# Moving the four block-diagonal copies of each q chunk from VectorE to SBUF-to-SBUF transfers, in an attention and MLP kernel with a fixed SyncE queue order

## The chip, the cores and the metric

The kernel runs on one core of one Trainium2 chip. The metric is the device time of one execution in microseconds (us), as the median of several runs. All timed runs quoted here were in the fast state; on one core that means that no run was more than 1.5% above the fastest run of the same kernel. (m1_shapes alone was run once, so its state is unknown; nothing is concluded from its time.) Ratios are computed as the mean time of one kernel's fast runs over that of the kernel before in the same rounds, so a ratio isn't quite the ratio of the medians quoted beside it. PE is TensorE, DVE is VectorE, ACT is ScalarE, SP is SyncE, which issues nearly all transfers here.

## The reference

Two layers, each of a local dilated attention and a token-mixing MLP, both with a residual (S = 2048 tokens, D = 1024, 32 heads of 32, window 8, dilation 2, F = 3584):

```python
def _A_ref(x, wqkv, wo):                       # attention
    H = 32; Dh = D // H; W, dil = 8, 2
    q, k, v = split_heads(x @ wqkv)            # cut: reshapes
    idx = pos[:, None] - dil * arange(W)[None, :]
    logits = einsum("bhsd,bhswd->bhsw", q, k[idx]) * Dh ** -0.5   # cut: mask of idx < 0
    o = einsum("bhsw,bhswd->bhsd", softmax(logits), v[idx])
    return merge_heads(o) @ wo

def _B_ref(x, w1, b1, w2, b2):                 # MLP over the tokens
    u = gelu(einsum("bsd,sf->bdf", layernorm(x), w1) + b1)
    return (einsum("bdf,fs->bds", u, w2) + b2).transpose(0, 2, 1)

for _ in range(2):
    x = x + _A_ref(layernorm(x), A_wqkv, A_wo)
    x = x + _B_ref(layernorm(x), B_w1, B_b1, B_w2, B_b2)
```

## The kernel before

One attention layer is cut into 16 units: a group of four heads (128 partitions, 32 per head) times one parity of the tokens. A unit has two visits (b = 0 and b = 1) of some 4.45 us each: 16 score matmuls, the value matmuls of the visit before, and two projection chunks for the next unit. In b = 0 these are the two q chunks, in b = 1 the two k chunks. Each q chunk is cast from PSUM to a tile `qs` by ACT, and then each head's 32 partitions are put into the head's own slot of `qB`. All else in `qB` is zero, so one matmul gives the scores of four heads apart.

```python
    def qk_chunk(u, wts, part, n):
        ...                                    # cut: 8 matmuls of 128x512 into ps
        ls = slice(n * 512, (n + 1) * 512)
        if part:
            nc.scalar.copy(out=kT[u % 2][:, ls], in_=ps[:])
        else:
            qs = x2("qs", [P, 512])            # shared pool of 6 buffers
            nc.scalar.copy(out=qs[:], in_=ps[:])
            for h in range(HG):                # 4 heads
                hp = slice(h * DH, (h + 1) * DH)
                nc.vector.tensor_copy(out=qB[u % 2][hp, h, ls], in_=qs[hp, :])
        return mm

    def scores(u, b):
        q, k = qB[u % 2], kT[u % 2]
        ...
        for i in range(HB):                    # 4 blocks of 128 tokens
            lo = (b * HB + i) * P
            for r in range(P // KG):           # 4 groups of 32 keys
                mm = nc.tensor.matmul(dst, lhsT=k[:, lo + r * KG:lo + (r + 1) * KG],
                                      rhs=q[:, :, lo + r * KG:lo + r * KG + GW], ...)   # GW = 40
        ...

    def out_proj(c, i, oT, wo, res, dst, h2):
        xr = x2("xr")                          # same pool
        nc.sync.dma_start(out=xr[:], in_=res(c, i))
        xn = x2("xn")                          # same pool
        for n in range(NDC):
            ...                                # 8 matmuls
            nc.vector.tensor_tensor(out=xn[:, xs_], in0=ps[:], in1=xr[:, xs_], op=ALU.add)
        nc.sync.dma_start(out=rows(dst, c, i), in_=xn[:])
        ...                                    # layernorm of xn into h2

        for vis in range(2 * NU):              # 32 visits of a layer
            u, b = divmod(vis, 2)
            if b == 0 and u + 1 < NU and (u + 1) % (2 * DIL) == 0:
                load_qk(...)                   # two loads of 512 KB
            if vis == 2 * NU - 6:
                wo = load_wo()                 # four loads of 512 KB
            in_order(scores, u, b)
            if vis:
                in_order(values, *divmod(vis - 1, 2), v, oT)
            for n in range(2):
                if u + 1 < NU:
                    in_order(qk_chunk, u + 1, wts, *chunks[2 * b + n])
                else:
                    in_order(out_proj, 0, 2 * b + n, oT, wo, res, xa[li], h2)
```

The last of the 16 matmuls of visit b = 0 reads columns 480 to 520, and so the first eight columns of the second q chunk. The second chunk is thus wanted when the unit starts, not half a unit later.

The softmax here doesn't subtract the row's maximum and nothing guards it: scores larger than these inputs give would overflow.

Of the kernel before, what the change touches and what calls it, by code (L numbers as in the profile page):

```python
# [12 lines left out]
BF16 = mybir.dt.bfloat16  # L13

P = 128
# [3 lines left out]
DIL = 2  # L19
# [6 lines left out]
def kernel(  # L26
# [15 lines left out]
    nc = tc.nc  # L42
# [9 lines left out]
    NG = D // P  # L52
    HG = P // DH
    NDC = D // 512
    FB = 256
# [13 lines left out]
    def pool(name, bufs, **kw):  # L69
        return ctx.enter_context(tc.tile_pool(name=name, bufs=bufs, **kw))  # L70
# [6 lines left out]
    wp = pool("wp", 9)  # L77
    x2p = pool("x2p", 6)
    pcp = pool("pcp", 2)
    dram = pool("dram", 1, space=bass.MemoryType.DRAM)  # L80
    psm = pool("psm", 2, space=bass.MemoryType.PSUM)
    pss = pool("pss", 2, space=bass.MemoryType.PSUM)
# [20 lines left out]
    def x2(name, shape=None, dt=BF16):  # L103
        return x2p.tile(shape or [P, D], dt, name=name, tag="x2")

    def wt_(name, shape):
        return wp.tile(shape, BF16, name=name, tag="w")
# [41 lines left out]
    qB = [pers.tile([P, HG, SC + W], BF16, name=f"qB{n}") for n in range(2)]  # L149
# [15 lines left out]
    wo_v = A_wo.rearrange("(g p) n -> p g n", p=P)  # L165
    w1_v = B_w1.rearrange("(i p c) f -> c p i f", p=P, c=DIL)
# [31 lines left out]
    last = {}  # L198

    def chain_(eng, f, *args):  # L200
        with tc.issue_after(last[eng].ins) if eng in last else nullcontext():
            last[eng] = f(*args)
# [138 lines left out]
    def load_qk(g2, ts):  # L341
        for part in range(2):
            ts[part] = wt_("wqk", [P, KD, 256])
            r = nc.sync.dma_start(out=ts[part][:], in_=wq_v[:, :, part * D + g2 * 256:part * D + (g2 + 1) * 256])
        return r

    def qk_chunk(u, wts, part, n):
        g, c = divmod(u, DIL)
        ps = m_tile()
        lo = c * SC + n * 512  # L350
        for kt in range(KD):
            mm = nc.tensor.matmul(ps[:], lhsT=wts[part][:, kt, (g % 2) * P:(g % 2 + 1) * P], rhs=hT[:, kt, lo:lo + 512],  # L352
                                  start=(kt == 0), stop=(kt == KD - 1))
        ls = slice(n * 512, (n + 1) * 512)
        if part:
            nc.scalar.copy(out=kT[u % 2][:, ls], in_=ps[:])  # L356
        else:
            qs = x2("qs", [P, 512])
            nc.scalar.copy(out=qs[:], in_=ps[:])  # L359
            for h in range(HG):  # L360
                hp = slice(h * DH, (h + 1) * DH)
                nc.vector.tensor_copy(out=qB[u % 2][hp, h, ls], in_=qs[hp, :])  # L362
        return mm

    last_pe = [None]
# [61 lines left out]
        nc.vector.tensor_tensor(out=oT[g][:, lo:lo + HB * P], in0=acc[:, 0, :], in1=rd[:], op=ALU.mult)  # L427
        return mm

    def load_wo():  # L430
        tiles = []
        for n in range(NDC):
            tiles.append([])
            for hf in range(2):
                t = wt_("wo", [P, NG // 2, 512])
                nc.sync.dma_start(out=t[:], in_=wo_v[:, hf * (NG // 2):(hf + 1) * (NG // 2), n * 512:(n + 1) * 512])
                tiles[n].append(t)
        return tiles

    def out_proj(c, i, oT, wo, res, dst, h2):  # L440
        xr = x2("xr")
        nc.sync.dma_start(out=xr[:], in_=res(c, i))
        xn = x2("xn")
        for n in range(NDC):
            ps = m_tile()
            xs_ = slice(n * 512, (n + 1) * 512)
            for g in range(NG):
                mm = nc.tensor.matmul(ps[:], lhsT=oT[g][:, cols(c, i)], rhs=wo[n][g // 4][:, g % 4, :],  # L448
                                      start=(g == 0), stop=(g == NG - 1))
            nc.vector.tensor_tensor(out=xn[:, xs_], in0=ps[:], in1=xr[:, xs_], op=ALU.add)  # L450
        nc.sync.dma_start(out=rows(dst, c, i), in_=xn[:])
        h2[c][i] = vhp.tile([P, D], BF16, name="h2", tag="vh")
        mean, rs = stats(xn, 1.0 + EPS, eps2)
        norm_act(h2[c][i][:], xn[:], mean, rs)
        return mm

    order = [(c, i) for c in range(DIL) for i in range(NI)]

    def load_w1(fb):
        tiles = []  # L460
        for c in range(DIL):
            t = wt_("w1", [P, NI, FB])
            nc.sync.dma_start(out=t[:], in_=w1_v[c, :, :, fb * FB:(fb + 1) * FB])
            tiles.append(t)
        return tiles

    def gemm1(fb, h2, g):
        wt = load_w1(fb)
        pairs = []
        g[fb] = gop.tile([P, GF, D], BF16, name="g", tag="go")  # L470

        def mm(fl, k):
            c, i = order[k]
            for dc in range(NDC):
                nc.tensor.matmul(pairs[fl][0][dc], lhsT=wt[c][:, i, fl * P:(fl + 1) * P],  # L475
                                 rhs=h2[c][i][:, dc * 512:(dc + 1) * 512], start=(k == 0), stop=(k == NT - 1))

        def gelu(fl):
            ft = fb * GF + fl
            aps, t = pairs[fl]  # L480
            if t is not None:
                nc.scalar.activation(out=g[fb][:, fl, :].rearrange("p (n d) -> p n d", n=2), in_=t[:],  # L482
                                     func=ACT.Gelu_apprx_tanh, bias=b1_sb[:, ft:ft + 1])
            else:
                for dc in range(NDC):
                    nc.scalar.activation(out=g[fb][:, fl, dc * 512:(dc + 1) * 512], in_=aps[dc],
                                         func=ACT.Gelu_apprx_tanh, bias=b1_sb[:, ft:ft + 1])

        for fl in range(GF):
            pairs.append(pair(fb * GF + fl))  # L490
        if fb == 0:
            for k in range(NT):
                for fl in range(GF):
                    mm(fl, k)
            for fl in range(GF):
                gelu(fl)
        else:
            for fl in range(GF):
                for k in range(NT):
                    mm(fl, k)  # L500
                gelu(fl)

    def load_w2(i):
        tiles = []
        for n in range(NW2):
            t = wt_("w2", [P, HF, 256])
            nc.sync.dma_start(out=t[:], in_=w2_v[:, n * HF:(n + 1) * HF, i * 256:(i + 1) * 256])
            tiles.append(t)
        return tiles
# [19 lines left out]
    NU = NG * DIL  # L529
    for li in range(2):  # L530
        first = li == 0
        v = [[None] * NI for _ in range(DIL)]
        for c, i in order:
            v[c][i] = vhp.tile([P, D], BF16, name="v", tag="vh")
        wv = load_wv()
        if first:
            start_up(v, wv)
            wts = [None, None]
            chain_("SP", load_qk, 0, wts)
            res = lambda c, i: xin_v[c, i]  # L540
        else:
            fill_wv(wv, 0)
            fill_wv(wv, 1)
            wts = [None, None]
            load_qk(0, wts)
            for i in range(NI):
                for c in range(DIL):
                    v_proj(v, c, i, wv, (0, 1))
            res = lambda c, i: rows(xb, c, i)
        oT = [gop.tile([P, S], BF16, name="oT", tag="go") for _ in range(NG)]  # L550
        h2 = [[None] * NI for _ in range(DIL)]
        chunks = [(0, 0), (0, 1), (1, 0), (1, 1)]
        last_pe[0] = None
        for part, n in chunks:
            in_order(qk_chunk, 0, wts, part, n)
        wo = None
        for vis in range(2 * NU):
            u, b = divmod(vis, 2)
            if b == 0 and u + 1 < NU and (u + 1) % (2 * DIL) == 0:
                wts = [None, None]  # L560
                load_qk((u + 1) // (2 * DIL), wts)
            if vis == 2 * NU - 6:
                wo = load_wo()
            in_order(scores, u, b)
            if vis:
                in_order(values, *divmod(vis - 1, 2), v, oT)
# [3 lines that stand above are left out]
                else:  # L570
                    in_order(out_proj, 0, 2 * b + n, oT, wo, res, xa[li], h2)
        in_order(values, NU - 1, 1, v, oT)
        for c, i in order[4:]:
            out_proj(c, i, oT, wo, res, xa[li], h2)
        g = [None] * NFB
        for fb in range(NFB):
            gemm1(fb, h2, g)
        if first:
            ln_exp_table()
        for i in range(NI):  # L580
            w2t = load_w2(i)
            for c in range(DIL):
                gemm2(c, i, w2t, g, xa[li], rows(xb, c, i) if first else out_v[c, i], first)

# [29 lines left out]
```

## Time and profile before

| | before |
|---|---|
| time, median of 3 runs (lowest to highest) | 1305.25 us (1304.77 to 1306.91) |
| span of the profiled run, granted TensorE clock | 1303.6 us, 1.0 |
| PE busy | 1278.7 us (98%) |
| DVE busy | 454.4 us (35%), 72.6 us of it the copies into qB |
| PE waits for DVE xn in the output projection | 7.3 us |

From the page of the kernel before: the busy time of each engine (us, share of the span, instructions), and the first line of the chain of work that ended last.

```profile
PE 1278.7 (98%) x8258; PEld 592.9 (45%) x8414; DVE 454.4 (35%) x971; ACT 372.4 (29%) x628; POOL 2.4 (0%) x15
...
PE 95%; DMA 2%; DVE 2%; issue 1%; ACT 1%; DVEq 0%; SPq 0%
```

PE is both the busiest engine and nearly all of the chain. What the other engines do costs nothing until PE waits for it. Three groups of instructions follow (line, engine, operation, output<-inputs, shapes, count | busy us, mean ns of one | idle us of the engine before them).

```profile
L352 PE MATMUL m<-hT,wqk 128*128 128x512 bf16 x963 | 223.4, 379 | 6.2 <-issue 4.6
...
L362 DVE COPY qB<-qs 32x512 bf16<-32x512 bf16 x256 | 72.6, 284 | 77.5 <-ACT qs L359 73.4
...
L380 PE MATMUL s<-qB,kT 128*32 128x160 bf16 x1024 | 29.5, 235 | 0.1
```

The score matmuls are 29.5 us of work and never wait (0.1 us). The "issue" idle time of the first line is no wait at all: 963 of 1024 matmuls have a record in this trace, and a missing record looks like a gap. From the view of PE's waits, by what it waited for (us in total, times, longest us):

```profile
PE m L448 <- DVE xn L450: 7.3, 6, 2.0
...
PE m L352 <- issue: 4.6, 29, 0.2
```

The timeline around the longest of these waits (start us, duration us, engine, work, [idle before <- what ended it]):

```profile
226.02 2.82 SPq L442 DMA_DIRECT2D xr<-in_A_x_dram  x2
...
230.66 1.29 DVE L450 TENSOR_TENSOR xn<-m,xr 128x512 bf16<-128x512 f32 x2 [2.64 <-DMA xr<-in_A_x_dram]
...
231.41 0.81 PE L448 MATMUL m<-wo,oT 128*128 128x512 bf16 x3 [1.98 <-DVE xn L450]
```

The residual tile xr is asked for when its tile starts; DVE sits idle 2.64 us for it, PSUM isn't emptied, and PE loses 1.98 us. Finally the timeline of an ordinary unit. The q chunks are cast, DVE copies them, and the next unit's scores come long after.

```profile
119.69 0.58 ACT L359 CAST qs<-m 128x512 bf16<-128x512 f32 x1 [0.35 <-PE m L352]
...
120.89 2.38 DVE L362 COPY qB<-qs 32x512 bf16<-32x512 bf16 x8
...
121.42 0.58 ACT L359 CAST qs<-m 128x512 bf16<-128x512 f32 x1 [1.14 <-PE m L352]
...
125.72 0.46 PE L380 MATMUL s<-qB,kT 128*32 128x160 bf16 x16
```

The eight copies end at 120.89 + 2.38 = 123.27, and the scores that read them start at 125.72: the copies have 2.45 us to spare.

### The profile page before, as it was taken

The numbers are of one execution on the slowest core, as the hardware profiler recorded it, in microseconds if no ns is written. First come the engines' busy times: TensorE is split into PE (matmuls) and PEld (weight loads), VectorE is DVE, ScalarE is ACT, GpSimd is POOL, SyncE is SP. The second block draws the span as 40 slices with busy tenths as digits, with TensorE's granted clock in tenths as the row PEclk, the third lists the DMA queues.
The fourth block names the chain that finished last, engine by engine and source line by source line (L and its number), as shares of the span: only waits on it lengthen the run. The fifth ranks groups of instructions, "written<-read, shape, count | busy, mean of one in ns | idle before, by whom it ended". The sixth has DMA issues, their size and how long they took to land.

```text
span 1303.6 us, 19189 instructions
## 1 busy us (share of the span) xinstructions
PE 1278.7 (98%) x8258; PEld 592.9 (45%) x8414; DVE 454.4 (35%) x971; ACT 372.4 (29%) x628; POOL 2.4 (0%) x15
## 2 busy tenths in 40 slices
PE   9999999999999999999999999999999999999998
PEld 4444444444444444444444444444444444444443
DVE  7468888820000013322300788888000000111111
ACT  5356665431111110000023666654211111000000
POOL 0000000000000000000000000000000000000000
PEclk9999999999999999999999999999999999999999
DMA  8620113452223236465432101034522222334330
GB/s 236 134 76 18 34 34 105 139 154 82 80 65 88 60 94 153 123 153 146 129 81 64 35 23 29 18 130 155 145 65 81 81 60 73 109 105 137 113 92 32
DMA packets 195812, 121.58 MB, mean 93 GB/s; under 512 B 37904, under 2 KB 177424, under 8 KB 195728
## 3 DMA queue, kind: packets, MB, share of 16 engines
q1 hardware_dynamic: 195728, 120.36, 32.6%
q8 instruction: 65, 1.06, 0.3%
q14 instruction: 19, 0.16, 0.0%
HBM read 96.48 MB, written 16.78 MB: 87 GB/s over the span
## 4 chain that ended last, share of the span: by engine, by line
PE 95%; DMA 2%; DVE 2%; issue 1%; ACT 1%; DVEq 0%; SPq 0%
PE m L352 17%; PE s L518 15%; PE s L475 15%; PE acc L475 7%; PE m L475 7%; PE m L518 7%; PE acc L518 7%; PE m L448 6%; PE m L337 4%; PE m L255 4%; PE s L380 2%; PE acc L408 1%; DMA xr<-in_A_x_dram 1%; PE acc L412 1%; DMA xr<-xb 1%
## 5 line engine op out<-in xcount | busy, mean ns | idle before, releaser
L518 PEld LDWEIGHTS <-w 128*128 128x128 bf16 x1792 | 175.3, 98 | 211.4
L475 PEld LDWEIGHTS <-w 128*128 128x128 bf16 x1792 | 175.3, 98 | 211.4
L352 PE MATMUL m<-hT,wqk 128*128 128x512 bf16 x963 | 223.4, 379 | 6.2 <-issue 4.6
L521 DVE SCALAR_TENSOR_TENSOR xo<-s,b_sb,xs 128x512 bf16<-128x512 f32 x32 | 24.0, 751 | 539.8 <-PE s L518 533.5
L475 PE MATMUL s<-h,w 128*128 128x512 bf16 x878 | 201.3, 379 | 0.8
L518 PE MATMUL s<-g,w 128*128 128x512 bf16 x884 | 199.3, 379 | 0.7
L352 PEld LDWEIGHTS <-wqk 128*128 128x128 bf16 x1024 | 95.2, 98 | 118.0 <-issue 10.7
L388 DVE TENSOR_TENSOR Pm<-pc,band 32x640 bf16<-32x640 bf16 x256 | 123.7, 483 | 46.0 <-ACT pc L383 39.2
L448 PE MATMUL m<-wo,oT 128*128 128x512 bf16 x500 | 111.9, 379 | 7.9 <-DVE xn L450 7.3
L475 PE MATMUL acc<-h,w 128*128 128x512 bf16 x440 | 103.1, 379 | 0.5
L518 PE MATMUL acc<-g,w 128*128 128x512 bf16 x436 | 99.7, 379 | 0.5
L362 DVE COPY qB<-qs 32x512 bf16<-32x512 bf16 x256 | 72.6, 284 | 77.5 <-ACT qs L359 73.4
L475 PE MATMUL m<-h,w 128*128 128x512 bf16 x438 | 98.5, 379 | 0.5
L518 PE MATMUL m<-g,w 128*128 128x512 bf16 x436 | 98.3, 379 | 0.6
L174 ACT ACTIVATE ln<-mv,eps 128x1 f32<-128x1 f32 x64 | 18.9, 295 | 244.2 <-DVE mv L182 238.8
L448 PEld LDWEIGHTS <-oT 128*128 128x128 bf16 x512 | 49.6, 98 | 68.6 <-issue 10.3
L482 ACT ACTIVATE g<-s,b_sb 128x1024 bf16<-128x1024 f32 x28 | 31.2, 1113 | 166.1 <-PE s L475 154.3
L255 PE MATMUL m<-wv,hT 128*128 128x512 bf16 x250 | 55.6, 379 | 1.0 <-ACT hT L249 0.7
L337 PE MATMUL m<-wv,hT 128*128 128x512 bf16 x251 | 55.2, 379 | 0.3
L359 ACT CAST qs<-m 128x512 bf16<-128x512 f32 x64 | 37.5, 585 | 51.4 <-PE m L352 50.3
L383 ACT ACTIVATE pc<-s,shift 128x640 bf16<-128x640 f32 x64 | 51.1, 799 | 0.0
L356 ACT CAST kT<-m 128x512 bf16<-128x512 f32 x64 | 37.5, 585 | 46.5 <-PE m L352 46.5
(57 smaller groups left out, 677.3 us busy)
## 6 DMA issues: line engine op xcount, KB each, us to landing
w<-in_B_w_dram SPq DMA_DIRECT2D x56, 512.0 KB, 3.8
w<-in_B_w_dram SPq DMA_DIRECT2D x64, 448.0 KB, 4.6
wqk<-in_A_wqkv_dram SPq DMA_DIRECT2D x16, 512.0 KB, 5.7
xa<-xn SPq DMA_DIRECT2D x32, 256.0 KB, 2.0
xs<-xa SPq DMA_DIRECT2D x32, 256.0 KB, 3.3
wv<-in_A_wqkv_dram SPq DMA_DIRECT2D x8, 512.0 KB, 5.2
wo<-in_A_wo_dram SPq DMA_DIRECT2D x8, 512.0 KB, 4.0
xr<-in_A_x_dram SPq DMA_DIRECT2D x16, 256.0 KB, 3.2
```

Source lines behind the costliest of these rows:

```text
L255: r = nc.tensor.matmul(pss_[k, n][:], lhsT=hT[:, kt, cols(*order[k])], rhs=wv[n][kt // 4][:, kt % 4, :], start=(kt == 0), stop=(kt == KD - 1))
L337: nc.tensor.matmul(ps[:], lhsT=hT[:, kt, cols(c, i)], rhs=wv[n][kt // 4][:, kt % 4, :], start=(kt == 0), stop=(kt == KD - 1))
L352: mm = nc.tensor.matmul(ps[:], lhsT=wts[part][:, kt, (g % 2) * P:(g % 2 + 1) * P], rhs=hT[:, kt, lo:lo + 512], start=(kt == 0), stop=(kt = ...
L356: nc.scalar.copy(out=kT[u % 2][:, ls], in_=ps[:])
L359: nc.scalar.copy(out=qs[:], in_=ps[:])
L362: nc.vector.tensor_copy(out=qB[u % 2][hp, h, ls], in_=qs[hp, :])
L383: nc.scalar.activation(out=pc[:].rearrange("p (n t) h k -> p n (t h k)", n=2), in_=ss[:, :, 0:2 * HG * GW], func=ACT.Exp, scale=scale, bia ...
L388: nc.vector.tensor_tensor(out=Pm[rp, :, s0:s0 + HB, r * KG:r * KG + GW].rearrange("p h t k -> p t h k"), in0=pc[rp], in1=mk, op=ALU.mult)
L448: mm = nc.tensor.matmul(ps[:], lhsT=oT[g][:, cols(c, i)], rhs=wo[n][g // 4][:, g % 4, :], start=(g == 0), stop=(g == NG - 1))
L475: nc.tensor.matmul(pairs[fl][0][dc], lhsT=wt[c][:, i, fl * P:(fl + 1) * P], rhs=h2[c][i][:, dc * 512:(dc + 1) * 512], start=(k == 0), stop ...
L482: nc.scalar.activation(out=g[fb][:, fl, :].rearrange("p (n d) -> p n d", n=2), in_=t[:], func=ACT.Gelu_apprx_tanh, bias=b1_sb[:, ft:ft + 1])
L518: nc.tensor.matmul(aps[dc], lhsT=w2t[ft // HF][:, ft % HF, c::DIL], rhs=g[ft // GF][:, ft % GF, dc * 512:(dc + 1) * 512], start=(ft == 0), ...
```

## The change

The intent is to relieve VectorE of the copies, to fix the order of SyncE's queue through attention so that the many small transfers meet known neighbours, and to take the residual loads out of the way of the output projection. Core of the diff:

```diff
+    qsp = pool("qsp", 2)
...
-            qs = x2("qs", [P, 512])
+            qs = qsp.tile([P, 512], BF16, name="qs", tag="qs")
             nc.scalar.copy(out=qs[:], in_=ps[:])
             for h in range(HG):
                 hp = slice(h * DH, (h + 1) * DH)
-                nc.vector.tensor_copy(out=qB[u % 2][hp, h, ls], in_=qs[hp, :])
+                chain_("SP", lambda: nc.sync.dma_start(out=qB[u % 2][hp, h, ls], in_=qs[hp, :]))
...
+    def load_xr(res):
+        t = x2("xr")
+        xrs.append(t)
+        chain_("SP", lambda: nc.sync.dma_start(out=t[:], in_=res(*todo.pop(0))))
...
     def out_proj(c, i, oT, wo, res, dst, h2):
-        xr = x2("xr")
-        nc.sync.dma_start(out=xr[:], in_=res(c, i))
+        xr = xrs.pop(0)
+        if todo:
+            load_xr(res)
...
-            if b == 0 and u + 1 < NU and (u + 1) % (2 * DIL) == 0:
-                wts = [None, None]
-                load_qk((u + 1) // (2 * DIL), wts)
-            if vis == 2 * NU - 6:
-                wo = load_wo()
+            if b == 0 and u % (2 * DIL) == 1 and u + 3 < NU:
+                nxt = [None, None]
+                chain_("SP", load_qk, u // (2 * DIL) + 1, nxt)
+            if b == 0 and (u + 1) % (2 * DIL) == 0 and u + 1 < NU:
+                wts = nxt
+            if vis == 2 * NU - 8:
+                wo = []
+                chain_("SP", load_wo, wo)
+            if vis == 2 * NU - 3:
+                todo[:] = order
+                load_xr(res)
+                load_xr(res)
...
-        for c, i in order[4:]:
+        for k, (c, i) in enumerate(order[4:]):
+            if k in (2, 4):
+                chain_("SP", load_w1, k // 2 - 1)
             out_proj(c, i, oT, wo, res, xa[li], h2)
```

`chain_("SP", f)` makes what f issues follow, on SyncE, what was chained there before. The change thus has two parts: the transfers in place of the copies, and the order with the early residual loads.

More of the change, by code (lines that the diff above doesn't have):

```diff
@@ L428, in values, with load_wo @@
         return mm
-    def load_wo():
-        tiles = []
+    def load_wo(tiles):
         for n in range(NDC):
@@ L435, in load_wo @@
                 t = wt_("wo", [P, NG // 2, 512])
-                nc.sync.dma_start(out=t[:], in_=wo_v[:, hf * (NG // 2):(hf + 1) * (NG // 2), n * 512:(n + 1) * 512])
+                r = nc.sync.dma_start(out=t[:], in_=wo_v[:, hf * (NG // 2):(hf + 1) * (NG // 2), n * 512:(n + 1) * 512])
                 tiles[n].append(t)
-        return tiles
+        return r
+    xrs, todo = [], []
+    def load_xr(res):
+        t = x2("xr")
+        xrs.append(t)
+        chain_("SP", lambda: nc.sync.dma_start(out=t[:], in_=res(*todo.pop(0))))
     def out_proj(c, i, oT, wo, res, dst, h2):
-        xr = x2("xr")
-        nc.sync.dma_start(out=xr[:], in_=res(c, i))
+        xr = xrs.pop(0)
+        if todo:
+            load_xr(res)
         xn = x2("xn")
@@ L462, in load_w1 @@
             t = wt_("w1", [P, NI, FB])
-            nc.sync.dma_start(out=t[:], in_=w1_v[c, :, :, fb * FB:(fb + 1) * FB])
+            r = nc.sync.dma_start(out=t[:], in_=w1_v[c, :, :, fb * FB:(fb + 1) * FB])
             tiles.append(t)
-        return tiles
+        w1s[fb] = tiles
+        return r
+    w1s = {}
     def gemm1(fb, h2, g):
-        wt = load_w1(fb)
+        if fb not in w1s:
+            load_w1(fb)
+        wt = w1s[fb]
         pairs = []
@@ L544 @@
             wts = [None, None]
-            load_qk(0, wts)
+            chain_("SP", load_qk, 0, wts)
             for i in range(NI):
@@ L572 @@
         in_order(values, NU - 1, 1, v, oT)
-        for c, i in order[4:]:
+        for k, (c, i) in enumerate(order[4:]):
+            if k in (2, 4):
+                chain_("SP", load_w1, k // 2 - 1)
             out_proj(c, i, oT, wo, res, xa[li], h2)
         g = [None] * NFB
+        last.pop("SP")
         for fb in range(NFB):
@@ L581 @@
             w2t = load_w2(i)
+            w1s.clear()
             for c in range(DIL):
```

## The prediction

> **What bounds the kernel.** TensorE. Busy: PE 1278.7 of 1303.6 us (98%), DVE 35%, ACT 29%; granted clock 1.0 in all slices; the chain is 95% PE. So what the change takes from VectorE is off the chain: the 256 copies qB<-qs cost 72.6 us of DVE, but no PE group waits for them. In the timeline (117 to 126 us) they end at 123.27; the scores that read them start at 125.72.
>
> PE's waits view: out_proj's matmuls wait for DVE xn 7.3 us in 6 waits, the longest 2.0; the qk chunks 4.6 us "issue" (29 gaps). Only the 7.3 us can be won. Their cause is the residual load: the chain has DMA xr pieces of 4.43, 3.50, 4.55 us (layer 1), 4.48, 3.68 (layer 2), because the queue issues xr behind the W1 loads that wait for PE (waits of the queue: up to 30.9 us), and xr is asked for only when its tile starts.
>
> **What the change does.**
> 1. xr is issued before the four tiles inside attention, and later ones two or more tiles ahead (built order: four xr loads before the first xa store). The DVE idle times for xr (6.7 us in all) go. Not all of the 7.3 us goes: at 209.70 to 210.39 DVE is busy with the mask and oT, so the first xn can start only about 1 us earlier (PE waits 0.3 instead of 1.3), the second 0.4 earlier; the third (1.98) vanishes. From the timeline: 3.7 us in layer 1, about 1.8 in layer 2. With issue gaps: 5.5 to 6.5 us won.
> 2. DVE loses 72.6 us: worth about 0.
> 3. 256 transfers of 32 KB join the queue. Issues cost 0.33 to 0.43 us each (timeline of SP), so the eight of a unit take about 3 of its 8.9 us; the queue fits. Landing: the smallest transfers now take 2.0 to 2.4 us. The second chunk's cast ends at 122.00; four issues put its last start near 123.3 and its landing near 125.3; it is needed near 126.1. Slack 0.8 us: hidden, barely.[...] Behind wo (four 512 KB loads, 3.5 to 7.2 us each) and wqk it may come late: estimate 0 to 2 us per layer.
> 4. Scores now wait on eight DMA semaphores instead of one of DVE. The built program has 100 semaphore-wait instructions on PE instead of 6; in the trace such an instruction takes 51 ns there. Two per unit follow full-length matmuls (partly hidden), one stands among the small score matmuls. Estimate: 94 x 51 ns = 4.8 us at most, about 2.5 exposed.
>
> **Sum.** 1305.25 - 6 + 2.5 + 1.5 = about 1303. I predict 1303.0 us, range 1297.0 to 1313.0; chances: faster by over 2% 0.01, within 2% 0.93, slower by over 2% 0.06.
>
> **Right if:** the waits of PE on DVE xn drop from 7.3 to under 2 us and DMA xr leaves the chain; DVE busy falls to about 382 us; a unit in attention stays at 8.9 to 9.1 us; qB landing is 1.6 to 2.2 us.
>
> **Wrong if:** landing of the qB transfers takes over 3 us or an issue over 0.6 us: then each of 30 units stalls, and 1 us each makes +30 us (slower). The sign: PE s L381 waiting for DMA qB, and a longer unit. If waits cost PE nothing and xn is freed fully: 1297.

The sum: 1305.25 - 6 + 2.5 + 1.5 comes to 1303.25, which it rounds to 1303.

## The result, and the profile after

| | before | after |
|---|---|---|
| time, median of 6 runs each (lowest to highest) | 1305.17 us (1304.77 to 1306.91) | 1340.05 us (1339.1 to 1343.61) |
| ratio, 95% interval | | 1.027 (1.0257 to 1.0284): slower |
| span of the profiled run, clock | 1303.6 us, 1.0 | 1337.4 us, 0.998 |
| DVE busy | 454.4 us | 384.2 us |
| PE waits for transfers into qB | none | 29.6 us |
| PE waits for DVE xn | 7.3 us | 3.3 us |

The kernel became slower by 2.7%, and lies outside the predicted range of 1297 to 1313. From the page after, the same parts as shown of before, and the line of the transfer issues (KB each, median us from issue to landing):

```profile
PE 1285.0 (96%) x8258; PEld 594.0 (44%) x8414; DVE 384.2 (29%) x715; ACT 376.0 (28%) x628; POOL 2.4 (0%) x15
...
PE 81%; DMA 7%; SPq 4%; ACT 3%; issue 2%; DVE 2%; another core or an unknown queue 0%; DVEq 0%; ACTq 0%
...
L381 PE MATMUL s<-qB,kT 128*32 128x160 bf16 x1024 | 36.7, 235 | 31.2 <-DMA qB<-qs 29.6
...
qB<-qs SPq DMA_DIRECT2D x256, 32.0 KB, 1.9
```

DVE's 70 us are gone, as intended, and PE's share of the chain fell from 95% to 81%: transfers and SyncE's queue stand in the chain now. The score matmuls, which never waited, wait 31.2 us. Their busy time rose too, from 29.5 to 36.7 us, though the mean of one stayed at 235 ns: where the sixteenth matmul is held back, it no longer overlaps the fifteen before it (all sixteen took 0.46 us in the unit shown of before; in the same unit below, fifteen take 0.46 us and the sixteenth 0.23 us by itself). PE's waits after:

```profile
PE s L381 <- DMA qB<-qs: 29.6, 31, 2.9
...
PE m L456 <- DVE xn L458: 3.3, 6, 1.1
PE s L381 <- ACT kT L357: 1.4, 2, 0.7
```

The 31 waits are one for nearly each of the 32 units of the two layers. The view of the tile qB tells what an issue costs (duration in ns as least/median/most, first and last start, count), and how long a transfer takes to land:

```profile
L363 SPq DMA_DIRECT2D qB<-qs x256: 507/589/1554, 68.3 to 884.7; - x128
...
DMA to landing us min/median/max: 1.7/1.9/5.6
```

Each issue holds SyncE for 589 ns (the median). The timeline of the same ordinary unit that was shown of before:

```profile
118.42 0.59 ACT L360 CAST qs<-m 128x512 bf16<-128x512 f32 x1 [0.38 <-PE m L353]
...
119.03 4.94 SPq L363 DMA_DIRECT2D qB<-qs  x8
...
120.14 0.59 ACT L360 CAST qs<-m 128x512 bf16<-128x512 f32 x1 [1.14 <-PE m L353]
...
124.45 0.46 PE L381 MATMUL s<-qB,kT 128*32 128x160 bf16 x15
...
125.40 0.23 PE L381 MATMUL s<-qB,kT 128*32 128x160 bf16 x1 [0.49 <-DMA qB<-qs]
```

Eight issues take 4.94 us; in the steady part of the train one starts every 0.633 us, which is 0.589 and a gap of 0.044 (by the single records). The four of the first chunk take about 4 x 0.633 = 2.53 us, but the second cast ends only 1.72 us after the first, so the second chunk's issues wait for SyncE, not for their data. By the single records the second cast ends at 120.73, the last issue starts at 123.38, 2.65 us later, and lands 1.88 us after that, at 125.26. The sixteenth score matmul wanted it at about 124.9: it starts 0.49 us late. The fifteen that need only the first chunk run on time.

The first unit of layer 1 shows a second cost:

```profile
72.81 0.46 PE L381 MATMUL s<-qB,kT 128*32 128x160 bf16 x15
...
76.12 0.23 PE L381 MATMUL s<-qB,kT 128*32 128x160 bf16 x1 [2.85 <-DMA qB<-qs]
...
76.51 5.09 PE L353 MATMUL m<-hT,wqk 128*128 128x512 bf16 x15 [0.16 <-issue]
```

After a wait of 2.85 us, fifteen projection matmuls take 5.09 us. In the ordinary unit fifteen of them take 3.40 us. The clock records of the trace show half clock here from 76.98 to 80.39 us, a stretch of 3.413 us. In these records the clock changes after whole numbers of such steps: the stretches at full clock before and after it, of 71.680 and 1256.105 us, are 21 and 368 steps of 3.4133 us, and the one of the kernel before, of 1297.065 us, is 380.

Where the time went can be added up against experiment e1 below, which has all of the change but the transfers (profiled spans 1302.0 and 1337.4 us, a difference of 35.4 us): waits for qB 29.6, the split score groups 36.7 - 29.5 = 7.2, waits for kT 1.4, the half clock about 1.7 (an estimate: half of its 3.413 us), and the waits for xn 3.3 - 5.4 = -2.1. That is 37.8 us, some 2 us more than the difference. The 7.2 us are too much: the held-back sixteenth matmul overlaps the value matmuls that follow it (in the unit above both start at 125.40 us). By the distance of the units the split costs less: three ordinary units of layer 1 start 9.57 to 9.60 us after the unit before them, and the same three in e1 8.91 to 8.97 us. Of the 0.65 us between them 0.49 us are the wait, so about 0.15 us a unit, some 5 us in all, belong to the split. With that the sum comes to about 35.4 us (an estimate from ordinary units).

The 29.6 us of waits are of three sorts. The first units of the two layers wait 2.85 and 1.46 us; in the first unit of layer 1 the scores start 4.46 us after the first issue, and in the ordinary unit 5.42 us, so there is about 1 us less to hide the train in. Of the other 30 units, 14 wait 1.24 us on average (17.4 us), and 16 wait 0.49 us on average (7.9 us in sum; one of them doesn't wait, and one waits 1.05 us). The 14 are those in whose stretch the trace has a transfer of the queue that the page calls q8, "instruction" (65 to 66 of them in a whole execution, before and after alike). All ten issues of more than 0.65 us (0.93 to 1.55 us) stand within 0.5 us of such a transfer, as 49 of all 256 do, and landings of 2.2 to 3.6 us lie there too. The same is seen in the other traces: of 133 issues into qB on SyncE that took over 0.8 us, in the eleven runs that have them, 118 started within 0.5 us of such a transfer, against 236 of all 2432 issues. No experiment moved these transfers, so this is a coincidence in time, though a close one, and not a shown cause.

In the output projection the order did its work only in part. In the kernel after, DVE now waits for something else:

```profile
264.27 0.69 DVE L458 TENSOR_TENSOR xn<-m,xr 128x512 bf16<-128x512 f32 x1 [1.53 <-DMA xa<-xn]
```

The residual is there, but the tile for the new xn isn't free: an earlier xn is still being stored. xr and xn share one pool of six buffers, and the residuals loaded ahead hold more of them.

### The profile page after: what moved, and what is told of

It is laid out like the page before. It is cut to its first block, busy times and chain, and to the rows that moved or that the text cites. A ratio compares the mean times of both kernels' runs of the same rounds, so it can differ in the third digit from the quotient of the medians.

```text
span 1337.4 us, 19460 instructions
## 1 busy us (share of the span) xinstructions
PE 1285.0 (96%) x8258; PEld 594.0 (44%) x8414; DVE 384.2 (29%) x715; ACT 376.0 (28%) x628; POOL 2.4 (0%) x15
## 4 chain that ended last, share of the span: by engine, by line
PE 81%; DMA 7%; SPq 4%; ACT 3%; issue 2%; DVE 2%; another core or an unknown queue 0%; DVEq 0%; ACTq 0%
PE s L531 14%; PE s L488 14%; PE m L353 8%; PE acc L488 7%; PE m L488 7%; PE m L531 7%; PE acc L531 7%; PE m L456 6%; DMA qB<-qs 4%; PE m L338 4%; PE m L256 4%; SPq L363 4%; ACT pc L384 1%; DMA wo<-in_A_wo_dram 1%; ACT rd L425 1%
## 5 line engine op out<-in xcount | busy, mean ns | idle before, releaser
L495 ACT ACTIVATE g<-s,b_sb 128x1024 bf16<-128x1024 f32 x28 | 31.2, 1114 | 166.9 <-PE s L488 155.2
L381 PE MATMUL s<-qB,kT 128*32 128x160 bf16 x1024 | 36.7, 235 | 31.2 <-DMA qB<-qs 29.6
```

## The experiments

The first theory was that the train of issues on SyncE is too long by half a microsecond in each unit (issue-bound). Rivals were that the landing, the waiting instructions on PE, or the other transfers around it (weight loads) cause the loss. All kernels gave correct results. Diffs are against the kernel after, unless another is named.

### e1_dve_copies: all of the change but the transfers

```diff
-                chain_("SP", lambda: nc.sync.dma_start(out=qB[u % 2][hp, h, ls], in_=qs[hp, :]))
+                nc.vector.tensor_copy(out=qB[u % 2][hp, h, ls], in_=qs[hp, :])
```

> The changed kernel with the four transfers per chunk put back to four DVE copies; the fixed queue order, the early residual loads and the own pool for qs stay. Theory A (the transfers are the whole loss: eight issues of 0.63 us each on one queue end too late for the scores): PE's waits for qB go to 0, PE waits for DVE xn stay at 3.3 us, time 1300 to 1302 us, 4 to 5 us under the kernel before. Rival R (the new queue order or the early residual loads cost the time): the time stays over 1320 us.

Measured: 1303.81 us (1302.58 to 1305.13), ratio 0.9984 (0.997 to 0.9997). From its groups, its PE waits and its timeline:

```profile
L381 PE MATMUL s<-qB,kT 128*32 128x160 bf16 x1024 | 29.5, 235 | 0.0
```

```profile
PE m L456 <- DVE xn L458: 5.4, 6, 2.0
```

```profile
245.83 0.69 DVE L458 TENSOR_TENSOR xn<-m,xr 128x512 bf16<-128x512 f32 x1 [2.60 <-DMA xa<-xn]
...
246.58 2.75 PE L456 MATMUL m<-wo,oT 128*128 128x512 bf16 x12 [1.59 <-DVE xn L458]
```

The whole loss belongs to the transfers: with the copies back on DVE the score matmuls wait 0.0 us. The expectation was right in this and missed the rest: the time is above its 1300 to 1302 us, because the waits for xn didn't stay at 3.3 us but are 5.4 us. The other half of the change is worth about 2 us (0.16% of 1305), not the 5.5 to 6.5 us predicted, since the wait for the residual became a wait for a store (2.60 us of DVE, 1.59 us of PE).

### b1_before_dma: the transfers without the order

The kernel before, with only the copies replaced (diff against before):

```diff
-                nc.vector.tensor_copy(out=qB[u % 2][hp, h, ls], in_=qs[hp, :])
+                nc.sync.dma_start(out=qB[u % 2][hp, h, ls], in_=qs[hp, :])
```

> The kernel before with the four transfers per chunk alone: no fixed queue order, no early residual loads. Theory A says that the transfers cost what they cost in the changed kernel, plus the old residual waits (7.3 instead of 3.3 us): 1343 to 1350 us; and if the scheduler places q transfers behind W1 or wqk loads that wait for PE, far more (over 1400 us), in which case the fixed order was needed for the transfers to work at all.

Measured: 1349.77 us (1349.13 to 1351.69), ratio 1.0347 (1.0332 to 1.0361). PE's waits:

```profile
PE s L380 <- DMA qB<-qs: 25.7, 26, 2.0
PE m L448 <- DVE xn L450: 11.7, 6, 3.5
```

The transfers alone cost about 45 us (3.47%), with the order 35 us. So the fixed order is worth some 10 us beside the transfers, mostly in the waits for xn (11.7 against 3.3 us; the expectation had put 7.3 there, so its time came out right with one part wrong), and some 2 us without them. The trace of b1 also has three stretches at half clock in its body, where sixteen projection matmuls take 5.31, 4.91 and 5.23 us instead of 3.61 to 3.63; that of the kernel after has one. It repairs a harm that the transfers themselves do.

### m1_shapes: what an issue costs

The kernel e1 with trains of eight transfers (four of the last kind) of several kinds added behind the attention of layer 2, where they touch tiles that nothing reads afterwards. Excerpt:

```diff
+            for n in range(8):
+                chain_("SP", lambda: nc.sync.dma_start(out=dst[n][0:32, :], in_=src[0:32, 0:512]))
...
+            for n in range(8):
+                chain_("SP", lambda: nc.sync.dma_start(out=dst[n][64:96, :], in_=x_in[n * 32:(n + 1) * 32, 0:512]))
+            for n in range(8):
+                chain_("SP", lambda: nc.sync.dma_start(out=sx[n * 32:(n + 1) * 32, 0:512], in_=src[0:32, 0:512]))
```

> A measurement inside e1_dve_copies: ahead of the second MLP of layer 2, when the tiles of attention are free, SP issues rows of eight transfers of one shape: SBUF to SBUF with 32 partitions of 1 KB (as qB<-qs), with 32 partitions of 128 bytes, with 96 partitions of 1 KB, with 16 partitions of 1 KB; HBM to SBUF with 32 partitions; SBUF to HBM with 32 partitions, and four with 128. The results stay right. Asked: why an issue of qB<-qs takes 0.589 us where the loads and stores that the prediction took as its measure took 0.33 to 0.43. If it is SBUF at both ends, all four SBUF-to-SBUF rows show 0.5 to 0.6 us and the HBM rows 0.33 to 0.43; if it is back-to-back issue, all rows show 0.5 to 0.6; if it is the number of partitions, the 96-partition row costs clearly more than the 16-partition one.

Measured in one look (1307.41 us, correct). Issues as in the view of a tile; the first line is from SBUF to SBUF, the second from DRAM to SBUF, the third from SBUF to DRAM, all 32 partitions of 1 KB:

```profile
L602 SPq DMA_DIRECT2D qB<-kT x8: 507/588/618, 901.6 to 906.6; - x8
...
L610 SPq DMA_DIRECT2D qB<-in_A_x_dram x8: 411/417/582, 924.8 to 928.2; - x8
...
L612 SPq DMA_DIRECT2D sx<-kT x8: 308/419/504, 928.7 to 932.2; - x8
```

| transfer | median issue, us |
|---|---|
| SBUF to SBUF, 32 partitions of 1 KB | 0.588 |
| SBUF to SBUF, 32 partitions of 128 bytes | 0.589 |
| SBUF to SBUF, 96 partitions of 1 KB | 0.593 |
| SBUF to SBUF, 16 partitions of 1 KB | 0.587 |
| DRAM to SBUF, 32 partitions of 1 KB | 0.417 |
| SBUF to DRAM, 32 partitions of 1 KB | 0.419 |
| SBUF to DRAM, 128 partitions of 2 KB | 0.45 |

In these trains an issue with both ends in SBUF takes 0.59 us, whatever the bytes and the partitions (a second train of the first kind, at partitions 96 to 127, had a median of 0.558); with one end in DRAM, 0.42 to 0.45. The figures hold for such trains and not for every issue: the issue of a wo load took 0.37 us in the kernel before (median) and 0.51 us in the kernel after, where SyncE also issues the q transfers; why was not tested. This is why the prediction's term was wrong: the kernel before has no plain transfer with both ends in SBUF (only 27 transposing ones, which took 1.23 to 1.25 us an issue in the median), and its SP timeline, from which the figure of 0.33 to 0.43 us was read, shows only loads and stores. Landing agrees with the prediction: 1.9 us in the median for the first kind.

### e3_dve_half and e5_extra: fewer and more issues per unit

Half of the copies back on DVE leaves four issues per unit, two behind each cast:

```diff
-                chain_("SP", lambda: nc.sync.dma_start(out=qB[u % 2][hp, h, ls], in_=qs[hp, :]))
+                if h < 2:
+                    nc.vector.tensor_copy(out=qB[u % 2][hp, h, ls], in_=qs[hp, :])
+                else:
+                    chain_("SP", lambda: nc.sync.dma_start(out=qB[u % 2][hp, h, ls], in_=qs[hp, :]))
```

> The changed kernel with heads 0 and 1 copied by DVE and heads 2 and 3 transferred: four issues per unit on SP, two behind each cast, in place of eight; chunk order and load queue as in the changed kernel. Theory A: the second chunk's last issue starts 0.6 us after its cast and lands 2.5 us after it, where the scores want it 3.7 to 4.1 us after it: no wait for qB in ordinary units or beside instruction fetches (which add about 0.8 us), and only 0 to 2 us per layer behind the four wo loads. PE waits for qB 0 to 5 us, time 1302 to 1310 us. If one transfer's landing were the trouble, waits stay over 10 us.

The 0.8 us for instruction fetches is the difference of the waits of 1.24 and 0.49 us in the kernel after, and a coincidence in time only.

Two more issues behind each cast, into a tile that nobody reads, make twelve per unit:

```diff
+            for h in range(2 * n, 2 * n + 2):
+                hp = slice(h * DH, (h + 1) * DH)
+                chain_("SP", lambda: nc.sync.dma_start(out=scr[hp, :], in_=qs[hp, 0:256]))
```

> The changed kernel with two useless transfers more per chunk (32 partitions of 512 bytes to an unused tile), behind the four that matter: twelve issues per unit in place of eight. Theory A (issue time of 0.63 us each adds up on the one queue): the second chunk's last needed issue starts 1.26 us later in every unit, so PE's waits for qB grow by about 1.2 us x 31, from 29.6 to 60 to 75 us, and the time to 1370 to 1395 us. If issues were not the limit (landing alone), these small transfers behind the needed ones change it by under 5 us.

Measured: e3 1303.17 us (1300.43 to 1306.6), ratio 0.9988 (0.9962 to 1.0013); e5 1405.11 us (1401.46 to 1408.75), ratio 1.0764 (1.0741 to 1.0788). PE's waits for qB, e3 and then e5:

```profile
PE s L384 <- DMA qB<-qs: 0.4, 1, 0.4
```

```profile
PE s L386 <- DMA qB<-qs: 66.4, 34, 2.8
```

Four, eight and twelve issues per unit give waits of 0.4, 29.6 and 66.4 us, while the median landing stays at 1.9 us in all three. The waits of e5 lie in the expected range, its time above it: the profiled run has a mean granted clock of 0.98 over 1401.2 us, so about 28 us were lost to the lower clock (an estimate from these two numbers). In e3 the landings are as slow as in the kernel after (1.7 to 5.3 us, median 1.9) and cost nothing. The length of the train decides, as the issue-bound theory says. In these runs an issue on SyncE was off the critical path up to the point where the train no longer fitted between the cast and the use (0.4 us of waits with four); from there further issues showed (29.6 us with eight, 66.4 us with twelve).

### e2_act_half: two issuing engines

```diff
+                if h < 2:
                     chain_("SP", lambda: nc.sync.dma_start(out=qB[u % 2][hp, h, ls], in_=qs[hp, :]))
+                else:
+                    nc.scalar.dma_start(out=qB[u % 2][hp, h, ls], in_=qs[hp, :])
```

> Heads 2 and 3 are transferred from ACT's queue, heads 0 and 1 from SP's. Theory A, if each queue pays its own 0.63 us per issue: last issue starts about 0.7 us after the cast, lands at 2.6 us, stall gone except behind the weight loads: PE waits for qB under 8 us, 1302 to 1312 us, and ACT busy by about 1.3 us more per chunk in issues, which may delay its casts a little.[...]

Measured: 1313.85 us (1311.51 to 1314.9), ratio 1.0057 (1.0044 to 1.0071). PE's waits:

```profile
PE s L384 <- ACT kT L357: 6.2, 8, 1.9
...
PE s L384 <- DMA qB<-qs: 2.9, 3, 1.1
```

The waits for qB fall from 29.6 to 2.9 us, as expected: a train of half the length is in time. Issues don't get slower when both engines make them (medians of 0.58 us on SyncE and 0.52 us on ACT), so the expectation's rival is out. (Its estimate was about 1.2 us an issue when both engines issue, and a time over 1325 us.) The time lies just above its 1302 to 1312 us. But ACT holds 0.52 us for each issue it makes, its own casts of k come late, and PE waits 6.2 us for these. Splitting the issues moves a part of the cost to an engine with work of its own in the same unit.

### e4_merged: four transfers per unit instead of eight

Both casts write one wide tile, and after the second each head goes with one transfer of 64 KB:

```diff
+            qs = qss[0]
+            nc.scalar.copy(out=qs[:, ls], in_=ps[:])
+            if n:
+                for h in range(HG):
+                    hp = slice(h * DH, (h + 1) * DH)
+                    chain_("SP", lambda: nc.sync.dma_start(out=qB[u % 2][hp, h, 0:SC], in_=qs[hp, :]))
```

> Four transfers of 64 KB per unit instead of eight of 32 KB, all issued after the second cast; the same bytes. Theory A (issue time adds up): last issue starts about 1.9 us after the second cast, lands at about 3.9 us, scores want it at 3.7 us after it: PE waits for qB fall from 29.6 us to 3 to 12 us, time 1303 to 1318 us. Rival B (the bytes or the landing of 1.9 us are what is late, whatever the count): PE waits stay at 25 us or more and the time at 1333 us or more.

Measured: 1321.66 us (1318.25 to 1323.02), ratio 1.0116 (1.0102 to 1.013).

```profile
PE s L386 <- DMA qB<-qs: 16.0, 25, 1.3
```

The direction is right, the size a miss: waits of 16.0 us against the 3 to 12 expected. Four issues last 2.4 us in an ordinary unit and land about 2.0 us later, and they can't begin before the second cast. The ordinary unit still comes some 0.23 us late, and all sixteen score matmuls now wait, not the last alone. But such units make up only 3.0 us of the 16.0. The other 13.0 us are twelve waits of 0.42 to 1.33 us, seven of them behind trains of 3.2 to 3.5 us with a long issue in them; the expectation had not counted these. Merging did pay (twice the bytes at the same issue of 0.588 us, and waits of 16.0 us instead of 29.6), but only about half of the waits could be saved, because merging delays the first transfers.

### e6_lead: the q chunks one chunk earlier

If the train is late by 0.5 us, a chunk of 1.7 us more lead should hide it. The chunks of the next unit are shifted by one, so that both q chunks are done one chunk before the place they had. The loads of wqk are asked for one unit earlier too, since the first q chunk needs them sooner (left out of the excerpt):

```diff
+        in_order(qk_chunk, 1, wts, 0, 0)
...
-                    in_order(qk_chunk, u + 1, wts, *chunks[2 * b + n])
+                    j = 2 * b + n + 1
+                    un = u + 1 + j // 4
+                    if un < NU:
+                        in_order(qk_chunk, un, wt_of[un // (2 * DIL)], *chunks[j % 4])
```

> All eight transfers kept, but the order of the four qk chunks is moved by one: the first q chunk of unit u+2 is made at the end of unit u, so the second q chunk comes one chunk (1.7 us) earlier and the first no longer competes with it for the queue. Theory A (late by 0.5 to 0.8 us per unit, nothing else): PE waits for qB below 4 us, time 1300 to 1306 us. Rival D (the semaphore waits on PE, 94 more of them, or the transfers' traffic cost PE time by themselves): 5 us or more remain over e1_dve_copies although no wait for qB is left.

Measured: 1333.58 us (1326.44 to 1334.76), ratio 1.0199 (1.0176 to 1.0223). The expectation of 1300 to 1306 us failed. PE's waits, and the timeline at the weights of the output projection:

```profile
PE s L381 <- DMA qB<-qs: 22.1, 10, 5.1
```

```profile
190.84 2.23 SPq L436 DMA_DIRECT2D wo<-in_A_wo_dram  x4
...
193.17 7.90 SPq L363 DMA_DIRECT2D qB<-qs  x8
...
201.32 0.29 PE L381 MATMUL s<-qB,kT 128*32 128x160 bf16 x1 [5.09 <-DMA qB<-qs]
...
202.47 5.79 PE L353 MATMUL m<-hT,wqk 128*128 128x512 bf16 x16
```

In the ordinary units the theory held: they wait 0 us. There are ten waits left, and eight of them, 21.3 of the 22.1 us, stand behind weight loads (the other two, 0.43 and 0.35 us, come 20 us after the last load of wo landed). Four loads of 512 KB are issued from 190.84 on; the four q transfers issued at 193.17 to 194.99 land 7.5 to 6.2 us after their issue, instead of 1.9. PE waits 5.09 us, and then runs at half clock: sixteen matmuls take 5.79 us instead of 3.63. The profiled run has a mean granted clock of 0.992 over 1332.7 us, so about 10 us were lost to the lower clock (an estimate from these two numbers). The new places put the q transfers directly behind the loads. That is a new wait in place of the old one, and the first theory was not the whole story.

Two gaps of about 2 us were followed by half clock here (1.96 and 2.03 us), and so, by the slow matmuls behind them, were gaps of 1.83, 2.02 and 3.21 us in b1. Gaps of 1.98 us in the kernel before, 2.04 us in e1, 2.62 us in e13 and 3.48 us in b1 were not. So the length of a gap alone doesn't tell. In the traces of before and after, the place of the gap does: cut into steps of 3.413 us from the first clock record on, the gap of 2.85 us in after lays 2.72 us into one step, at whose end the half clock begins, while the gap of 1.98 us in before is cut into 1.43 and 0.55 us. But for the end of the program, no other step of these two traces has more than 1.53 us of idle time in it, and none is followed by half clock. This is one case, counted and not tested by an experiment; no limit follows from it.

### e8_lead_actloads, e13_lead_act_pinned and e14_lead_spread: loads on another queue, or apart in time

Is it that loads and q transfers share SyncE's queue, or that they are in flight together? e8 is e6 with the weight loads issued from ACT (diff against e6):

```diff
-            r = nc.sync.dma_start(out=ts[part][:], ...)
+            r = (nc.scalar if g2 else nc.sync).dma_start(out=ts[part][:], ...)
...
-                r = nc.sync.dma_start(out=t[:], in_=wo_v[...])
+                r = nc.scalar.dma_start(out=t[:], in_=wo_v[...])
```

> e6_lead, with the weight loads of attention (wqk of groups 1 to 3, and wo) issued from ACT's queue[...], in place of SP's. In e6_lead all ten waits for qB (22.1 us) stand behind such loads, up to 5.1 us, and the longest were followed by half clock. Theory E[...]: q landing beside loads falls from 3 to 7.5 us to under 3 us, waits for qB fall under 4 us, no half clock, time 1301 to 1307 us. If the loads delay q wherever they are issued from[...], waits stay over 15 us. What then remains over e1_dve_copies (1303.8) is the price of the 94 semaphore waits on PE: 0 to 5 us.

Theory E is that the shared queue delays the q transfers, its rival that the loads delay them from any queue.

Measured: 1302.84 us (1301.92 to 1304.11), ratio 0.9981 (0.9968 to 0.9995), waits for qB 1.1 us. But this run doesn't answer the question. Without the chain the loads also moved: in the trace the four of wo were issued at 67.7, 94.7, 99.1 and 130.1, one by one and long before, so queue and time changed together.

e13 is e6 with the loads on ACT, each pair or four tied to the cast before it, to keep them about where e6 has them (diff against e6):

```diff
-                chain_("SP", load_qk, u // (2 * DIL) + 1, nxt)
+                with tc.issue_after(cast[0].ins):
+                    load_qk(u // (2 * DIL) + 1, nxt)
...
-                chain_("SP", load_wo, wo)
+                with tc.issue_after(cast[0].ins):
+                    load_wo(wo)
```

> e6_lead with the weight loads of attention on ACT's queue, as in e8, but held at the place in time that they have in e6 (in e8 the scheduler moved most of them 10 to 60 us earlier and one by one, so that e8 changed two things). Theory E1 (the queue matters[...]): waits for qB fall from 22.1 us to under 6 us. Theory E2 (the time matters[...]): waits for qB stay at 12 us or more and the time at 1318 us or more. Four issues of wo ahead of an exponential on ACT may cost 1 to 2 us per layer by themselves.

The 1 to 2 us per layer for four issues on ACT are an estimate; four of 0.375 us, the median issue of a wqk load on ACT in e8, would be 1.5 us.

e14 is e6 with the loads still on SyncE, but one load of 512 KB per unit, just behind the second q chunk, so that it has most of a unit before the next q transfers (diff against e6):

```diff
-            if b == 0 and u % (2 * DIL) == 0 and u + 4 < NU:
-                nxt = [None, None]
-                chain_("SP", load_qk, u // (2 * DIL) + 1, nxt)
+            if b == 1 and u % (2 * DIL) < 2 and u // (2 * DIL) + 1 < NU // (2 * DIL):
+                nxt = wt_of.setdefault(u // (2 * DIL) + 1, [None, None])
+                chain_("SP", load_qk, u // (2 * DIL) + 1, nxt, (u % (2 * DIL),))
...
-            if vis == 2 * NU - 8:
-                wo = []
-                chain_("SP", load_wo, wo)
+            if b == 1 and 0 <= u - (NU - 6) < 4:
+                wo = wo or []
+                chain_("SP", load_wo, wo, (u - (NU - 6),))
```

> e6_lead with every load left on SP's queue, but each 512 KB issued by itself, one per unit, just behind the second q chunk, where the next q transfer is 5 us away. Theory E2 (time and size of the burst): one load lands in about 4 us, before the next q: waits for qB under 4 us, no half clock, time 1301 to 1306 us. Theory E1 (same queue is what hurts): waits stay over 12 us.

A wo load landed after 4.0 us in the kernel before and after 3.9 us in e8 (medians).

Measured: e13 1311.28 us (1309.07 to 1314.71), ratio 1.0051 (1.0032 to 1.007); e14 1302.42 us (1301.6 to 1302.57), ratio 0.9973 (0.9958 to 0.9988). PE's waits for qB in e13, and then in e14:

```profile
PE s L383 <- DMA qB<-qs: 2.3, 5, 1.1
```

```profile
PE s L381 <- DMA qB<-qs: 0.5, 1, 0.5
```

The landings of those q transfers that were issued while a weight load was in flight, read from the records:

| | such q transfers | median landing, us | longest, us |
|---|---|---|---|
| after | 28 | 2.8 | 5.6 |
| e6, loads in a burst on SyncE | 46 | 4.3 | 7.5 |
| e13, loads in a burst on ACT | 65 | 4.5 | 7.3 |
| e14, loads one by one on SyncE | 40 | 2.5 | 3.8 |

In e13 the queue differs and the landings are as slow as in e6. In e14 the queue is the same as in e6, and the landings are short. So in these runs it is the loads in flight that slow them, in a burst (4.3 and 4.5 us in the median) more than one by one (2.5 us); a second queue didn't shield them. Two flaws stay. In e14 the q transfers also follow a load's issue by 2.6 to 3.7 us, and in e6 by 0.6 to 2.3 us, so the number of loads in flight and the distance to them changed together. And the loads of e13 went 2.5 to 5 us earlier than in e6, so its shorter waits (2.3 against 22.1 us) may come from that and can't be booked as a merit of the queue. By the expectation's own signs (waits under 6 us, time under 1318 us) e13 spoke for the queue; it is the landings, and e14 with waits of 0.5 us on the same queue, that speak against it. The profiled e13 is 6.9 us longer than e14: 1.8 us of it are waits for qB, 2.8 us waits for DVE's oT (4.5 against 1.7), and 1.9 us busy time of PE; what makes oT late was not followed up. With e14, lead and spread loads, the transfers are hidden on SyncE alone.

### e9_x2p7, e10_w1_early and e12_lead_x2p7: the version that beats both, and what DVE's relief is worth

e9 has the order of the change, the copies on DVE as before, and seven buffers in the shared pool (qs back in it, its own pool gone):

```diff
-    x2p = pool("x2p", 6)
+    x2p = pool("x2p", 7)
-    qsp = pool("qsp", 2)
...
-            qs = qsp.tile([P, 512], BF16, name="qs", tag="qs")
+            qs = x2("qs", [P, 512])
...
-                chain_("SP", lambda: nc.sync.dma_start(out=qB[u % 2][hp, h, ls], in_=qs[hp, :]))
+                nc.vector.tensor_copy(out=qB[u % 2][hp, h, ls], in_=qs[hp, :])
```

> e1_dve_copies without the pool for qs (qs from the shared pool, as before), and that shared pool with 7 buffers in place of 6: in e1 the longest waits of the output projection (1.59 and 2.04 us) stand where xn waits for the store of an earlier xn to land. If the pool's size is what makes it wait, these two go and the time is 1299 to 1302 us; if not, it stays at 1303 to 1304.

e10 is e9 with three of the four first W1 loads brought into attention (diff against e9):

```diff
+            if vis == 2 * NU - 6:
+                chain_("SP", load_w1, 0)
+            if vis == 2 * NU - 4:
+                chain_("SP", load_w1, 1, (0,))
```

> e9_x2p7, with three of the first four W1 tiles loaded inside attention again and only one during the output projection, so that stores and residual loads do not stand behind 1 MB there. If the W1 loads make the store late, PE's waits for DVE xn fall from 5.4 to under 2.5 us and the time is 1298 to 1301 us; if they are harmless, it equals e9.

e12 is e8, so hidden transfers in place of the copies, with the same seven buffers:

```diff
-    x2p = pool("x2p", 6)
+    x2p = pool("x2p", 7)
-    qsp = pool("qsp", 2)
```

> e8_lead_actloads (transfers kept and hidden) with the pool of e9_x2p7 (7 shared buffers, qs among them). Both costs of the changed kernel are then gone and VectorE has 72 us less to do than in e9. If DVE relief is worth something, it lands under e9's 1300.2 by 1 us or more; if it is worth nothing, as the prediction said, it equals e9 within 1 us or is a little slower by the semaphore waits on PE: 1299 to 1302 us.

Measured: e9 1300.19 us (1299.63 to 1300.79), ratio 0.996 (0.9946 to 0.9973); e10 1300.29 us (1299.77 to 1300.43), ratio 0.996 (0.9948 to 0.9973); e12 1299.36 us (1298.84 to 1299.39), ratio 0.9957 (0.9944 to 0.9971). PE's waits for xn in e9:

```profile
PE m L455 <- DVE xn L457: 1.8, 4, 0.6
```

One more buffer takes DVE's waits for a store of xn from 5.7 us (e1) to none, PE's waits for xn from 5.4 us (e1) to 1.8 us, and the gain from about 2 to about 5 us: the wait for the store was the rest of what the prediction had promised for the early residuals. Earlier W1 loads add nothing (e10). And with the transfers hidden (PE still waits 0.8 us for them), the relief of VectorE is worth nothing that these runs resolve: the intervals of e12 and e9 cover each other. They differ in the place of the chunks and loads and in PE's waiting instructions too, so it is the sum of all these that is about 0. e9 is the simpler of the two, and beats the kernel before by 0.4%.

## Why the prediction was wrong

1. **Residual loads: mechanism right, size off.** Of the five pieces of DMA xr in the chain before (20.6 us) one is left in the chain after (2.80 us), nearly as predicted, but PE's waits for xn fell only to 3.3 us (after) and 5.4 us (e1), not under 2. The prediction looked at what xr waited for and not at what its buffers keep from others. The freed wait came back as a wait for the store of an earlier xn, because two residuals ahead take buffers out of a pool of six. With seven (e9) the waits are 1.8 us and the gain is about 5 us.
2. **VectorE's relief worth about 0: right.** DVE fell to 384.2 us (predicted: about 382), and e12 against e9 shows no value in it that these runs resolve.
3. **The transfers: the step that failed.** It reads "Issues cost 0.33 to 0.43 us each [...] four issues put its last start near 123.3 and its landing near 125.3 [...] Slack 0.8 us: hidden, barely." An issue took 0.589 us and 0.044 us of gap. The last issue began 2.65 us after the second cast's end, not 1.3: the first chunk's four weren't out in time (2.53 us for them, 1.72 us between the casts), and each of the second four was longer too. That is 1.35 us more than predicted against a slack of 0.8 us, so about 0.55 us late; measured 0.49 us in the ordinary unit. The prediction started the last four at the cast and left the first four, still in the same queue, out of the sum. So the stall came although the issue, at 0.589 us, stayed under the 0.6 us that it had named as the sign of failure. The landing, 1.9 us, was inside the predicted 1.6 to 2.2. The trace before, where the prediction read 2.0 to 2.4 us for the smallest transfers, has shortest landings of 2.0 us. The durations used for the issue were from another kind of transfer, as m1 showed.
4. **The size of the loss.** The prediction's own sign of failure came true in kind ("each of 30 units stalls"). 0.49 us in each of 32 units would be 16 us. The rest of the 35 us is three things that it didn't price: longer waits where an instruction load coincides (coincidence only), the split score group (some 5 us), and the first units with the half clock after.
5. **Behind the weight loads, "0 to 2 us per layer".** The mechanism was right. In the kernel after, q transfers near the loads landed after up to 5.6 us. In the units behind wo the waits for qB were 0.70 and 0.53 us. In e6, where they stood directly behind the loads, it was 21.3 us of waits in two layers, and about 10 us lost to the lower clock on top (an estimate).
6. **Waiting instructions on PE, estimated at 2.5 us: about 0.** e12 and e14 have the hidden transfers with PE waiting on their semaphores, and are at 1299.36 and 1302.42 us, against 1300.19 (e9) and 1303.81 (e1) with copies: no loss is to be seen. What these instructions cost and what VectorE's relief may bring can't be told apart here, so 0 is shown for both together only.

What stays open: whether the instruction loads lengthen the issues beside them, or merely coincide; and what part of the slow landings behind loads depends on the queue, on the number of loads in flight and on the distance to them, as e13 couldn't hold the loads in place exactly and e14 changed two of these at once.

## What to carry to other kernels

Cost a train of small transfers on its issuing engine first, with the issue duration of the same kind of transfer (SBUF to SBUF was 0.59 us in a train, not the 0.42 of a transfer with one end in DRAM), and set the whole train, and not one transfer's landing, against the time between the producer and the first reader. Moving work off an engine that is off the critical path earned nothing that could be measured here, and when it is moved, more lead helps less where a burst of large loads is in flight at the new place, as in e6. A tile that is loaded ahead takes a buffer from someone: look for the wait that appears next in the same pool.
